# Tie-free first cluster by triangle products, and other places for side work, in attention with two MLPs

## The chip, the cores and the metric

The kernel runs on one core of a Trainium2 chip. The metric is the device time of one execution in microseconds (us), the median of several runs. The engines of the core run side by side, each through its own queue of instructions in order: TensorE (PE, matrix products and transposes), VectorE (DVE), ScalarE (ACT), GpSimd (POOL) and SyncE (SP, which here starts DMA transfers). They wait for each other by semaphores.

## The reference, cut to what matters

Attention over 16 heads (768 tokens of 64) in which a query sees only the keys of its own cluster (the first of 16 centroids with the largest similarity), then a Fourier mixing with norm and an MLP, then a gated MLP with a convolution over the tokens:

```python
q_assign = np.argmax(np.einsum('bhsd,hcd->bhsc', q_n, c_n), axis=-1)
k_assign = np.argmax(np.einsum('bhsd,hcd->bhsc', k_n, c_n), axis=-1)
mask = q_assign[:, :, :, None] == k_assign[:, :, None, :]
scores = np.where(mask, scale * np.matmul(q, k.transpose(0, 1, 3, 2)), -1000000000.0)
attn = np.exp(scores - np.max(scores, axis=-1, keepdims=True))
attn = attn / (np.sum(attn, axis=-1, keepdims=True) + 1e-09)
x = np.matmul(attn, v)                       # heads side by side: 2 x 768 x 512
u = x + np.real(np.fft.fft(np.fft.fft(x, axis=1), axis=2))
un = (u - mu) / np.sqrt(var + 1e-06)
x = u + np.maximum(un @ w_ch1, 0.0) @ w_ch2  # w_ch1 is 512 x 2048
h = np.maximum(x @ w_in, 0.0)                # w_in is 512 x 1024
conv_out = sum(conv_w[k] * hp[:, k:k + S, :] for k in range(3))
gate = 1.0 / (1.0 + np.exp(-conv_out))
return h * gate @ w_out
```

`np.argmax` takes the first of equal values, so where two clusters of a token are equally near, the one with the lower number counts.

## The kernel before

**Attention.** The 16 heads are taken as 8 pairs `m`; each head has 6 tiles of 128 tokens, which makes 96 tiles, and the loop at the end of the attention part runs one step `n` per tile. Step `n` issues the scores of tile `n + 8` (`score_max`: four products at L612 and L614 into a PSUM slot, and VectorE's negated row maximum at L617), then the transposed scores of tile `n` with mask and maximum in the product (`score_exp`: L649, L651, and ScalarE's exponential at L657), then the products with V of tile `n - 3` (`attn_v`, 18 products at L689). The probabilities are kept as two 16-bit parts: the high part by ScalarE (`prob_hi`, L669), the low part, which is the difference, by VectorE or GpSimd (`prob_lo`, L677); the set `LO_ON_DVE` lists the tiles whose low part VectorE makes. Scores and transposed scores take turns in three PSUM slots, so the transposed scores of tile `n + 1` go into the slot that the scores of tile `n + 8` leave: they wait for that tile's maximum on VectorE, and for whoever reads the slot's spare columns 384 to 512.

**Side work in the attention steps.** Everything else is put between these steps by hand, by `at(place, step, function)`; the places of a step in their order are `pre`, `mid` (which gets the score tile's slot and uses its spare columns), `late`, `aft`, `post` and `fill`. For the pair `m`, that begins at step `k = 12 m - 24`, these are: the similarities to the centroids (`prep_sims`), their turn and row maximum and the marks of equality with it (`sims_turn`, L472 and L482); then the first of equal marks, by a weight that falls with the cluster's number (`prep_first` L486, `prep_pick` L490, `prep_mark` L496), four transposes and two ScalarE copies of the one-hot marks (`prep_turn`, L511) and a DMA of them to DRAM; the high and low parts of q and k (`prep_hi` L536, `prep_lo`); and V's scale and two parts (`v_max`, `v_turn`, `v_step`, whose step 5 at L594 is V's low part on VectorE). The first steps of the Fourier mixing of the first batch and the conversion of the first weights (`ahead0` to `ahead3`, `first_split`) lie in the later steps.

**After the attention** the code gives only data, pools and priorities: a scheduler orders the instructions of each engine. MLP1 has 16 blocks `f` per batch (`mlp1_up`, `down`), the gated MLP has 8 (`mlp2_up`: products, ReLU, convolution on VectorE at L992 and L993, sigmoid, product with the gate, two parts; then `down`). Weights come as 64-bit words by DMA (`load_w`; `B_LOADS` lists the blocks of MLP1's second batch after which those of the gated MLP are asked for), VectorE converts them (L301 to L306), and they are scaled and split in two 16-bit parts (`split_16`: ScalarE, then VectorE at L947). `gate_in` measures the tokens (L1040 to L1042), turns them (L1065) and splits them (L1068). The outputs leave through a buffer `y` of three tiles.

## Time and profile before

| | |
|---|---|
| median of three runs | 680.25 us (678.62 to 681.44) |
| the profiled execution, its own time | 679.71 us |
| its span in the trace | 677.9 us |
| TensorE busy | 656.7 us, 97% |
| VectorE busy | 546.0 us, 81% |
| ScalarE busy | 420.1 us, 62% |
| GpSimd busy | 181.2 us, 27% |

The profile is of one execution; its time is 1.8 us more than its span, and 0.54 us less than the median. Busy shares are means over the whole span. A wait in the trace is the idle time of an engine just ahead of an instruction, with the instruction that came last of those that it waited for.

### The profile page before, as it was taken

The page shows a single profiled execution, that of the slowest core. Times are in us where ns is not written, and L with a number is a line of the kernel's source. Part 1 is how long each engine was busy: PE and PEld are TensorE (multiplying, and loading weights), DVE is VectorE, ACT ScalarE, POOL GpSimd, SP SyncE. Part 2 cuts the span into 40 slices and gives each one's busy share as a digit, 9 for nine tenths or more (in the row PEclk, how much of TensorE's full clock was granted, in tenths as well). Part 3 has the DMA queues.
Part 4 walks back from the last instruction along what each step waited for, and adds up shares of the span by engine and source line. Part 5 has one row for each costly group of instructions (what it writes and reads, how often), then busy time and mean ns, then how long its engine had stood idle before and what let it go on. Part 6 is the DMA issues. An engine that isn't in the chain of part 4 may idle for free.

```text
span 677.9 us, 12606 instructions
## 1 busy us (share of the span) xinstructions
PE 656.7 (97%) x5019; PEld 487.8 (72%) x5019; DVE 546.0 (81%) x884; ACT 420.1 (62%) x679; POOL 181.2 (27%) x153
## 2 busy tenths in 40 slices
PE   8999999898999999999999999999999999999996
PEld 4888888786989888899999996554555555555553
DVE  6989999989878999998599838997626399867663
ACT  6688888786667895566246644776436276655442
POOL 8376866676648742000011000000000000000000
PEclk9999999998999999999999999999999999999999
DMA  6678788682644530334013330333000000002002
GB/s 191 179 165 206 192 222 220 149 194 51 177 110 90 143 122 2 125 125 155 33 62 125 125 124 1 125 125 126 1 1 0 1 1 1 0 2 80 14 1 93
DMA packets 21542, 65.41 MB, mean 96 GB/s; under 512 B 4438, under 2 KB 7306, under 8 KB 18668
## 3 DMA queue, kind: packets, MB, share of 16 engines
q1 hardware_dynamic: 20476, 60.86, 31.3%
q0 software_dynamic: 1008, 3.75, 2.0%
q8 instruction: 39, 0.64, 0.4%
q14 instruction: 19, 0.16, 0.1%
HBM read 40.84 MB, written 5.58 MB: 68 GB/s over the span
## 4 chain that ended last, share of the span: by engine, by line
PE 65%; DVE 25%; ACT 4%; DMA 2%; issue 2%; SPq 1%; POOL 0%; DVEq 0%; ACTq 0%
PE acc L87 7%; PE acc L86 7%; PE acc L85 7%; PE up L85 5%; PE up L87 5%; PE up L86 5%; DVE m L617 4%; PE av L689 4%; PE s L612 3%; DVE p L677 3%; PE s L614 3%; PE t L649 3%; PE t L651 2%; PE u L85 2%; PE u L87 2%; PE u L86 2%
## 5 line engine op out<-in xcount | busy, mean ns | idle before, releaser
L677 POOL TENSOR_TENSOR p<-p,p 128x768 f16<-128x768 f32 x61 | 106.7, 1752 | 73.3 <-ACT p L669 32.8
L657 ACT ACTIVATE p<-t,cbias 128x768 f32<-128x768 f32 x93 | 83.6, 900 | 21.9 <-PE t L651 19.9
L617 DVE TENSOR_REDUCE m<-s 128x1 f32<-128x768 f32 x96 | 90.3, 946 | 5.6 <-PE s L614 3.5
L669 ACT CAST p<-p 128x768 f16<-128x768 f32 x90 | 74.7, 830 | 1.2
L689 PE MATMUL av<-V,p 128*128 128x65 f16 x1728 | 70.6, 195 | 1.0 <-POOL p L677 0.9
L689 PEld LDWEIGHTS <-p 128*128 128x128 f16 x1728 | 59.1, 98 | 16.3 <-issue 15.0
L649 PE MATMUL t<-X 128*128 128x384 f32 x192 | 54.7, 366 | 4.6 <-DVE m L617 4.1
L612 PE MATMUL s<-X 128*128 128x384 f32 x192 | 56.5, 376 | 1.8 <-DVE eq L482 0.5
L614 PE MATMUL s<-Y 96*128 96x384 f32 x192 | 49.7, 340 | 0.1
L651 PE MATMUL t<-Y 98*128 98x384 f32 x192 | 49.8, 340 | 0.0
L85 PE MATMUL u<-x,wb 128*128 128x384 f16 x128 | 41.7, 326 | 1.3 <-DVE h L989 0.9
L85 PE MATMUL up<-un,wa 128*128 128x384 f16 x128 | 41.8, 326 | 0.7 <-DVE x L1068 0.3
L677 DVE TENSOR_TENSOR p<-p,p 128x768 f16<-128x768 f32 x32 | 40.8, 1276 | 1.1 <-ACT p L669 1.1
L86 PE MATMUL up<-un,wa 128*128 128x384 f16 x128 | 41.7, 326 | 0.0
L87 PE MATMUL u<-x,wb 128*128 128x384 f16 x128 | 41.7, 326 | 0.0
L86 PE MATMUL u<-x,wb 128*128 128x384 f16 x128 | 41.7, 326 | 0.0
L87 PE MATMUL up<-un,wa 128*128 128x384 f16 x128 | 41.6, 326 | 0.0
L649 PEld LDWEIGHTS t<-X 128*128 128x128 f32 x192 | 31.3, 190 | 10.4 <-DVE m L617 7.1
L85 PE MATMUL up<-un,wha 128*128 128x384 f32 x112 | 38.0, 339 | 0.0
L86 PE MATMUL up<-un,wha 128*128 128x384 f32 x112 | 37.8, 337 | 0.0
L87 PE MATMUL up<-un,wla 128*128 128x384 f32 x112 | 37.7, 338 | 0.0
L265 POOL TENSOR_TENSOR rs<-rs,half 128x1 f32<-128x1 f32 x12 | 10.5, 905 | 100.5 <-DVE rs L260 92.5
(397 smaller groups left out, 1698.5 us busy)
## 6 DMA issues: line engine op xcount, KB each, us to landing
rawa<-w SPq DMA_DIRECT2D x14, 1024.0 KB, 4.7
rawb<-w SPq DMA_DIRECT2D x8, 1024.0 KB
raw<-qk SPq DMA_DIRECT2D x7, 768.0 KB, 4.3
X<-G SPq DMA_DIRECT2D x13, 384.0 KB, 3.7
Y<-G SPq DMA_DIRECT2D x13, 384.0 KB, 5.0
vraw<-v SPq DMA_DIRECT2D x8, 384.0 KB, 5.4
out<-y SPq DMA_DIRECT2D x12, 256.0 KB, 3.1
X<-G SPq DMA_DIRECT2D x14, 192.0 KB, 4.1
```

The costliest lines, as they stand in the source:

```text
L85: T.matmul(o, sH, mH, start=start, stop=False)
L86: T.matmul(o, sH, mL, start=False, stop=False)
L87: T.matmul(o, sL, mH, start=False, stop=stop)
L612: T.matmul(t[:, c, 0:384], X[:, 0, sl], X[:, 1, 384 * c:384 * c + 384], start=True, stop=False)
L614: T.matmul(t[:, c, 0:384], Y[0:96, 0, sl], Y[0:96, 1, 384 * c:384 * c + 384], start=False, stop=True)
L617: V.tensor_reduce(m6s[h][:, i:i + 1], t[:, :, 0:384], AX.XY, ALU.max, negate=True)
L649: T.matmul(t[:, c, 0:384], X[:, 1, sl], X[:, 0, 384 * c:384 * c + 384], start=True, stop=False)
L651: T.matmul(t[:, c, 0:384], Y[0:98, 1, sl], Y[0:98, 0, 384 * c:384 * c + 384], start=False, stop=True)
L657: A.activation(p, t[:, :, 0:384], AF.Exp, bias=cbias, scale=0.125)
L669: A.copy(p16[:, 0], p32s[n])
L677: eng.tensor_sub(p16[:, 1], p, p16[:, 0])
L689: T.matmul(o, p16[:, k, 128 * j:128 * j + 128], v16[:, i, h % 2, 65 * part:65 * part + 65], start=(i + j + k + part == 0), stop=(i == 5), ...
```

## The change

- **First of equal marks.** For the pairs 2 to 7, `prep_first`, `prep_pick`, `prep_mark` and `prep_turn` are replaced. `equal_turn` transposes the marks of equality themselves (four transposes, one ScalarE copy of 96x512). `equal_sole` multiplies them with a constant matrix `sole` (1 for the cluster itself, -1 for those of lower number in the same token block, 0 elsewhere), two products per half; a mark stays over 0 only where no lower cluster is marked. The half `a = 0` is read by ScalarE (ReLU with a factor), the half `a = 1` by VectorE (`tensor_scalar`), each 96x256. They hang on the score tiles of steps `k + 7`, `k + 8` and `k + 9`, where there were `prep_first` to `prep_mark` and, at `k + 11`, `prep_turn`. The DMA of the marks is issued two steps earlier.
- **Low parts.** `LO_ON_DVE` has 28 tiles where it had 32, and mostly others: 3 of 12 per pair up to the fifth. The low parts of q and k of pair 7 go from VectorE to GpSimd, `first_split` 3 from GpSimd to VectorE. In the last tiles, 90 and 92 are VectorE's instead of 91 and 94.
- **V.** The maximum of |V| of the pairs 0 and 6 is taken by ScalarE (absolute value with a sum as a bound) where it was VectorE's. V's low part and other side work stand at other steps, by the table `MOVED`, which overrides place and step in `at`.
- **MLP1's end.** The gated MLP's blocks of weights from the sixth on are asked for one block `f` later (`B_LOADS`); its scales, and the first splits, one block later too.
- **Gated MLP.** The splits of its later weights, and `measure` of the second batch, are held back by `issue_after` until the gate products of earlier blocks are issued. `y` has six buffers instead of three.

```diff
-LO_ON_DVE = ({n for n in range(54) if n % 12 in (2, 7, 8, 10)}
-             | {54, 56, 59, 61, 62, 68, 73, 76, 80, 83, 86, 87, 88, 91, 94})
+LO_ON_DVE = {4, 7, 8, 14, 16, 19, 20, 28, 31, 32, 40, 43, 44, 52, 55, 57, 59, 61, 67, 68, 72, 77, 80, 82, 85,
+             88, 90, 92}
+LO_BY_DVE = ()
+ABS_ON_ACT = (0, 6)
+MOVED = {
+    ("prep_sims", 2): ("post", 5),
...
+    ("v_step", 5, 5): ("fill", 56),
...
-    NA, NB, B_LOADS = (2, 7, 7), (3, 5), (1, 2, 4, 5, 7, 8, 9, 10)
+    NA, NB, B_LOADS = (2, 7, 7), (3, 5), (1, 2, 4, 5, 7, 9, 10, 11)
...
+        sole = ep.tile([96, NT, C], F16, name="sole")
+        G.memset(sole, -1.0)
...
+        def sole_part(op, fill_, p, t, c):
+            G.affine_select(sole, sole, [[t, NT], [c, C]], op, fill_, base=0, channel_multiplier=p)
+
+        def equal_turn(m, t):
+            p = t[0:96, :, 384:512].bitcast(F16)
+            e = eqs[m].rearrange("p (h a t) c -> p h a (t c)", h=2, a=2)
+            for a in range(2):
+                for h in range(2):
+                    T.transpose(p[:, a, 128 * h:128 * h + 128], e[:, h, a], ident16)
+            s = sts[m] = ep.tile([128, 384], F32, tag="st", bufs=1, name=f"eT{m}")[0:96, 0:256].bitcast(F16)
+            s = sts[m] = s.rearrange("p (a n) -> p a n", a=2)
+            A.copy(s, p)
+
+        def equal_sole(m, a, t):
+            p = t[0:96, :, 384:512]
+            for h in range(2):
+                T.matmul(p[:, h], sole.rearrange("p t c -> p (t c)"), sts[m][:, a, 128 * h:128 * h + 128],
+                         start=True, stop=True)
+            if a == 0:
+                o = ohTs[m] = ep.tile([96, 2, 2, 128], F32, tag="ohT", bufs=1, name=f"ohT{m}")
+                A.activation(o[:, 0], p, AF.Relu, scale=BIG)
+            else:
+                V.tensor_scalar(ohTs[m][:, 1], p, 0.0, 1.0, ALU.max, ALU.subtract)
+                d = ohD[m] = dr.tile([96, 2, 2, 128], F32, tag="ohd", name=f"ohd{m}")
+                nc.sync.dma_start(out=d, in_=ohTs[m])
...
-            V.tensor_reduce(sc[:, 0:1], vraws[m], AX.XYZ, ALU.max, apply_absolute_value=True)
+            if m in ABS_ON_ACT:
+                junk = V16s[m % 2].bitcast(BF16).rearrange("p t h e -> p (t h) e")[:, :, 0:64]
+                A.activation(junk, vraws[m].rearrange("p t h d -> p (t h) d"), AF.Abs, accum_out=sc[:, 0:1])
+            else:
+                V.tensor_reduce(sc[:, 0:1], vraws[m], AX.XYZ, ALU.max, apply_absolute_value=True)
...
-                at(fill, k + 6, prep_first, m, V if m == 6 else G)
-                at(fill, k + 7, prep_pick, m)
-                at(fill if m == 7 else late, k + (7 if m == 7 else 8), prep_mark, m)
...
-                at(mid, k + 11, prep_turn, m)
...
+                for f, n in zip(((equal_turn, m), (equal_sole, m, 0), (equal_sole, m, 1)),
+                                (8, 9, 11) if m == 2 else (k + 7, k + 8, k + 9)):
+                    at(mid, n, *f)
...
-                (V, G)[i // 2].tensor_sub(w[i], src, f32(w[i - 1]))
+                V.tensor_sub(w[i], src, f32(w[i - 1]))
...
-        V.tensor_mul(t, t, hc)
+        gate_op.append(V.tensor_mul(t, t, hc).ins)
...
-            ws_b[f + 1] = split_16(gp, "b", f + 1)
+            with tc.issue_after(gate_op[f - 2]):
+                ws_b[f + 1] = split_16(gp, "b", f + 1)
...
-                    y = gps[0].tile([128, 512], F32, tag="y", bufs=3, name=f"y{g}{t}")
+                    y = gps[0].tile([128, 512], F32, tag="y", bufs=6, name=f"y{g}{t}")
...
+            with tc.issue_after(gate_op[min(t, len(gate_op) - 1)]) if b else nullcontext():
+                measure_(t)
...
-            if (g, f) == (1, 11):
+            if (g, f) == (1, 12):
                 scales("b")
...
-            if g == 1 and f >= 12 and f < 12 + NB[0]:
-                ws_b[f - 12] = split_16(wbp[0], "b", f - 12)
+            if g == 1 and f >= 13 and f < 13 + NB[0]:
+                ws_b[f - 13] = split_16(wbp[0], "b", f - 13)
```

What this does to the order of VectorE's instructions is shown at three places. A row is line, operation, written tile <- read tiles, and shape; line numbers are those of the kernel it is of (the score maximum is L617 before and L786 after, the low part L677 and L847, V's low part L594 and L763).

VectorE in the attention, around the score tiles 62 to 65, where the marks of pair 6 are made. Before:

```order
L472 TENSOR_REDUCE mx6_2541<-cols6_2516 128x24
L482 TENSOR_TENSOR eq6_2543<-cols6_2516,mx6_2541 128x384
L617 TENSOR_REDUCE m6_10_2433<-s62_2533 128x1
L486 TENSOR_TENSOR eq6_2543<-eq6_2543,desc_135 128x384
L617 TENSOR_REDUCE m6_10_2433<-s63_2575 128x1
L677 TENSOR_TENSOR p16_54_2581<-p54_2553,p16_54_2581 128x768
L594 SCALAR_TENSOR_TENSOR V16_1_155<-vraw5_2149,vsc5_2355,V16_1_155 128x12x64
L490 TENSOR_REDUCE m26_2610<-eq6_2543 128x24
L617 TENSOR_REDUCE m6_10_2433<-s64_2612 128x1
L496 TENSOR_TENSOR oh6_2627<-desc_135,m26_2610 128x384
L697 TENSOR_SCALAR d8_2651<-av8_2413 128x6
L617 TENSOR_REDUCE m6_10_2433<-s65_2653 128x1
```

After:

```order
L611 TENSOR_REDUCE mx6_2548<-cols6_2528 128x24
L621 TENSOR_TENSOR eq6_2550<-cols6_2528,mx6_2548 128x384
L786 TENSOR_REDUCE m6_10_2443<-s62_2540 128x1
L786 TENSOR_REDUCE m6_10_2443<-s63_2585 128x1
L786 TENSOR_REDUCE m6_10_2443<-s64_2625 128x1
L847 TENSOR_TENSOR p16_55_2635<-p55_2604,p16_55_2635 128x768
L763 SCALAR_TENSOR_TENSOR V16_1_157<-vraw5_2164,vsc5_2347,V16_1_157 128x12x64
L867 TENSOR_SCALAR d8_2667<-av8_2423 128x6
L676 TENSOR_SCALAR ohT6_2632<-s65_2669 96x256
L786 TENSOR_REDUCE m6_10_2443<-s65_2669 128x1
```

The three operations on the marks (L486, L490, L496) are gone, V's low part and the one low part of this stretch stand behind the maximum of tile 64 instead of ahead of it, and the new reading of the products (L676) stands ahead of that of tile 65.

VectorE in MLP1's second batch, around block 6 (`h1_6` is the ReLU's low part of that block, `wb6` the gated MLP's seventh block of weights, `cw` the convolution's weights, `x0` the turned tokens). Before:

```order
L301 TENSOR_SCALAR wb6_6502<-rawb6_6503 128x1024
L302 SCALAR_TENSOR_TENSOR wb6_6502<-rawb6_6503,wb6_6502 128x1024
L971 SCALAR_TENSOR_TENSOR h1_6_6155<-up1_6_0_6156,h1_6_6155 128x384
L971 SCALAR_TENSOR_TENSOR h1_6_6155<-up1_6_1_6171,h1_6_6155 128x384
L304 SCALAR_TENSOR_TENSOR wb6_6502<-rawb6_6503,wb6_6502 128x1024
L301 TENSOR_SCALAR cw_4486<-craw_6512 128x24
L306 SCALAR_TENSOR_TENSOR wb6_6502<-rawb6_6503,wb6_6502 128x1024
L1068 TENSOR_TENSOR x0_5844<-xT03_6207,x0_5844 128x4
L302 SCALAR_TENSOR_TENSOR cw_4486<-craw_6512,cw_4486 128x24
L304 SCALAR_TENSOR_TENSOR cw_4486<-craw_6512,cw_4486 128x24
L1068 TENSOR_TENSOR x0_5844<-xT03_6207,x0_5844 128x4x127
```

After:

```order
L438 TENSOR_SCALAR cw_4499<-craw_6515 128x24
L439 SCALAR_TENSOR_TENSOR cw_4499<-craw_6515,cw_4499 128x24
L441 SCALAR_TENSOR_TENSOR cw_4499<-craw_6515,cw_4499 128x24
L1150 SCALAR_TENSOR_TENSOR h1_6_6168<-up1_6_0_6169,h1_6_6168 128x384
L443 SCALAR_TENSOR_TENSOR cw_4499<-craw_6515,cw_4499 128x24
L1150 SCALAR_TENSOR_TENSOR h1_6_6168<-up1_6_1_6184,h1_6_6168 128x384
L1252 TENSOR_TENSOR x0_5857<-xT03_6220,x0_5857 128x4
L438 TENSOR_SCALAR wb6_6580<-rawb6_6581 128x1024
L1252 TENSOR_TENSOR x0_5857<-xT03_6220,x0_5857 128x4x127
L439 SCALAR_TENSOR_TENSOR wb6_6580<-rawb6_6581,wb6_6580 128x1024
```

The conversion of `wb6` stands behind both parts of `h1_6` instead of ahead of and around them, the small `cw` conversions ahead, and the last piece of `x0` stands behind the first step of `wb6`.

VectorE at the start of the gated MLP (`h200` and `h201` are the ReLU products of the first two blocks, `cv00` and `cv01` their convolutions, `wb3` to `wb5` splits of later weights, `tok1` the measures of the second batch). Before:

```order
L947 SCALAR_TENSOR_TENSOR wb3_6987<-wb3_6225,scb_6643,wb3_6987 128x512 x2
L947 SCALAR_TENSOR_TENSOR wb4_7036<-wb4_6359,scb_6643,wb4_7036 128x512
L989 SCALAR_TENSOR_TENSOR h200_6856<-u000_6859,x0_5844 128x384
L947 SCALAR_TENSOR_TENSOR wb4_7036<-wb4_6359,scb_6643,wb4_7036 128x512
L1040 TENSOR_REDUCE tok10_7055<-U_68 128x1
L1040 TENSOR_REDUCE tok11_7070<-U_68 128x1
L989 SCALAR_TENSOR_TENSOR h200_6856<-u001_6874,x0_5844 128x384
L1041 TENSOR_SCALAR tok10_7055<-tok10_7055 128x1
L1041 TENSOR_SCALAR tok11_7070<-tok11_7070 128x1
L947 SCALAR_TENSOR_TENSOR wb5_7123<-wb5_6430,scb_6643,wb5_7123 128x512
L1042 TENSOR_SCALAR tok10_7055<-tok10_7055 128x1
L1042 TENSOR_SCALAR tok11_7070<-tok11_7070 128x1
```

After:

```order
L1168 SCALAR_TENSOR_TENSOR h200_6869<-u000_6872,x0_5857 128x384
L1168 SCALAR_TENSOR_TENSOR h200_6869<-u001_6887,x0_5857 128x384
L1171 SCALAR_TENSOR_TENSOR cv00_6902<-h200_6869,cw_4499,cv00_6902 128x768
L1168 SCALAR_TENSOR_TENSOR h201_6913<-u010_6916,x0_5857 128x384
L1172 SCALAR_TENSOR_TENSOR cv00_6902<-h200_6869,cw_4499,cv00_6902 128x768
L1168 SCALAR_TENSOR_TENSOR h201_6913<-u011_6931,x0_5857 128x384
L1161 MEMSET h202_6957 128x1
L1162 MEMSET h202_6957 128x1
L1174 TENSOR_TENSOR cv00_6902<-cv00_6902,hc00_6868 128x768
L1171 SCALAR_TENSOR_TENSOR cv01_6946<-h201_6913,cw_4499,cv01_6946 128x768
L1126 SCALAR_TENSOR_TENSOR wb3_7000<-wb3_6238,scb_6710,wb3_7000 128x512
L1177 TENSOR_TENSOR gL00_6909<-cv00_6902,gH00_6908 128x768
```

The two blocks' own work now comes first; the splits of `wb4` and `wb5` and the measures have left this stretch for later ones, and that of `wb3` stands in two halves behind the first block's gate product.

## Rows read from the trace of the kernel before

**Rows 1.** The profile's first part: span, then busy time, share and instructions per engine.
```profile
span 677.9 us, 12606 instructions
...
PE 656.7 (97%) x5019; PEld 487.8 (72%) x5019; DVE 546.0 (81%) x884; ACT 420.1 (62%) x679; POOL 181.2 (27%) x153
```

**Rows 2.** TensorE's waits: tile and line that waits <- engine, line: us, times, longest.
```profile
PE t L649 <- DVE m L617: 4.1, 3, 2.8
PE s L621 <- DVE m L617: 1.6, 1, 1.6
...
PE xT L1065 <- DVE h L971: 1.0, 1, 1.0
PE av L689 <- POOL p L677: 0.9, 1, 0.9
PE u L85 <- DVE h L989: 0.9, 1, 0.9
```

**Rows 3.** Timeline of TensorE, three steps: start, us, instruction, shapes, [wait ahead of it <- releaser].
```profile
102.22 0.59 PE L612 MATMUL s<-X 128*128 128x384 f32 x2
...
104.64 0.60 PE L612 MATMUL s<-X 128*128 128x384 f32 x2
...
106.70 0.59 PE L612 MATMUL s<-X 128*128 128x384 f32 x2
```

**Rows 4.** Timeline of VectorE ahead of TensorE's longest wait, pair 6.
```profile
154.72 1.54 DVE L677 TENSOR_TENSOR p<-p,p 128x768 f16<-128x768 f32 x1
156.18 2.41 DVE L594 SCALAR_TENSOR_TENSOR V<-vraw,vsc,V 128x768 f16<-128x768 f32 x1
...
158.97 0.94 DVE L617 TENSOR_REDUCE m<-s 128x1 f32<-128x768 f32 x1
```

**Rows 5.** That wait on TensorE, and the stretch behind it (window, length, PE, PEld, DVE, ACT, POOL busy, granted clock).
```profile
159.97 1.01 PE L649 MATMUL t<-X 128*128 128x384 f32 x2 [2.80 <-DVE m L617]
...
163.67 0.59 PE L649 MATMUL t<-X 128*128 128x384 f32 x2
...
159.95:163.36 3.41, 3.40 (x25) 3.09 (x26) 3.03 (x6) 1.62 (x2) 0.29 (x1) 0.50 0.00 0
```

**Rows 6.** Timeline of VectorE, two low parts in pair 5.
```profile
127.91 2.59 DVE L677 TENSOR_TENSOR p<-p,p 128x768 f16<-128x768 f32 x1
...
131.37 0.94 DVE L677 TENSOR_TENSOR p<-p,p 128x768 f16<-128x768 f32 x1
```

**Rows 7.** Groups by line: count | busy us, mean ns of one | idle ahead, releaser.
```profile
L677 POOL TENSOR_TENSOR p<-p,p 128x768 f16<-128x768 f32 x61 | 106.7, 1752 | 73.3 <-ACT p L669 32.8 <-issue 26.2 <-PE t L651 5.7
L657 ACT ACTIVATE p<-t,cbias 128x768 f32<-128x768 f32 x93 | 83.6, 900 | 21.9 <-PE t L651 19.9 <-POOL ev L115 0.7 <-POOL eq L486 0.6
L669 ACT CAST p<-p 128x768 f16<-128x768 f32 x90 | 74.7, 830 | 1.2
```

**Rows 8.** TensorE's wait in pair 3, and ScalarE's copy that is its root.
```profile
75.74 0.58 PE L649 MATMUL t<-X 128*128 128x384 f32 x2 [0.87 <-DVE m L617]
...
70.90 0.83 ACT L536 CAST G<-raw 128x768 fp32r<-128x768 f32 x1 [0.85 <-DMA Y<-G]
```

**Rows 9.** MLP1: the late VectorE step, and a load of weights in the chain.
```profile
462.71 1.23 DVE L302 SCALAR_TENSOR_TENSOR wb<-rawb,wb 128x1024 int32<-128x1024 int32 x1
463.85 1.02 DVE L971 SCALAR_TENSOR_TENSOR h<-up,h 128x384 f16<-128x384 f32 x2
...
456.74 5.22 DMA rawb<-w
```

**Rows 10.** Busy time in the first 50 us of the gated MLP (columns as in rows 5).
```profile
550.00:600.00 50.00, 48.22 (x277) 26.94 (x275) 44.83 (x97) 32.75 (x56) 0.00 (x0) 1.00 0.00 1
```

**Rows 11.** Timeline of VectorE at the end: the last two outputs that it makes.
```profile
672.49 0.75 DVE L1020 TENSOR_SCALAR y<-acc,ysc 128x512 f32<-128x512 f32 x1 [1.46 <-DMA out<-y]
...
673.89 0.75 DVE L1020 TENSOR_SCALAR y<-acc,ysc 128x512 f32<-128x512 f32 x1 [0.65 <-ACT y L1022]
```

**Rows 12.** Timeline of ScalarE at the start, ahead of the first transposed scores.
```profile
21.81 0.79 ACT L639 CAST Y<-first_max 2x768 fp32r<-2x768 f32 x1 [6.67 <-PE first_max L637]
```

More of the change, by code (lines that the diff above doesn't have):

```diff
@@ L411, in tile_net @@
         add_stack(G)
-        sq = ep.tile([128, D], F32, name="sq")
+        sq = ep.tile([128, 192], F32, tag="eq", bufs=1, name="sq")[:, 0:D]
         V.tensor_mul(sq, cn, cn)
@@ L705, in tile_net, with at @@
         LEAD, LAG = 8, 3
-        pre, mid, late, aft, post, fill = {}, {}, {}, {}, {}, {}
-        def at(where, step, *f):
+        pre, mid, mid2, late, aft, post, fill = {}, {}, {}, {}, {}, {}, {}
+        hooks = dict(pre=pre, mid=mid, mid2=mid2, late=late, aft=aft, post=post, fill=fill)
+        def at(where, step, *f, name=None):
+            key = (name or f[0].__name__, *(x for x in f[1:] if isinstance(x, int)))
+            if key in MOVED:
+                where, step = MOVED[key]
+                where = hooks[where]
             where.setdefault(step, []).append(f)
@@ L739, in tile_net @@
         at(fill, -3, first_split_max, 0)
+        for f in ((ALU.is_ge, 0.0, 1, -C, 0), (ALU.is_ge, 0.0, -1, C, 1), (ALU.not_equal, 1.0, -1, C, 1)):
+            at(fill, -4, sole_part, *f)
         at(fill, -2, prep_pick, 1)
@@ L774, in tile_net @@
         for name, where, n in plan:
-            at(where, n, first[name])
+            at(where, n, first[name], name=name)
         stat, root, scale, swap, low = norm(0, lambda name: slot(name)[:, 0], dp)
@@ L794, in ahead_start @@
             dst = ahead[q] = t[:, 2560 + 512 * q:3072 + 512 * q]
-            for n, op in zip(AHEAD_STEPS[5 * q:], from64(dst, raw)):
-                at(aft, n, op)
+            for i, (n, op) in enumerate(zip(AHEAD_STEPS[5 * q:], from64(dst, raw))):
+                at(aft, n, op, name=f"ahead{q}_{i}")
         def ahead_store(q):
@@ L897, in tile_net @@
                 score_exp(n)
+            for f in mid2.get(n, []):
+                f[0](*f[1:], tile_s)
             for f in late.get(n, []):
```

147 lines of the change are left out of this document (141 added, 6 removed).

## Prediction

> **What bounds the kernel now.** I read the profile's first part, then TensorE's waits, then the stretch around each wait on the engines it names. TensorE is busy 656.7 of 677.9 us [rows 1], so 21 us are all that filling its gaps can give, some of it at the start and end; a change gains here by the waits it takes from TensorE and loses by what it adds to TensorE's work or to the waits. In the attention VectorE is the usual releaser: the transposed scores wait 4.1 us for the score maximum, the turn of the maxima 1.6, one product with V 0.9 for GpSimd's low part [rows 2]. After it come single waits of about a microsecond for VectorE's h [rows 2]. No wait is spread over all steps: a free step is bound by TensorE and takes 2.06 us, from 104.64 to 106.70 [rows 3].
>
> The longest wait shows the pattern. At 159.97 TensorE had stood for 2.80 us [rows 5]; VectorE had made a low part of 1.54 us and V's low part of 2.41 us between two maxima, and the maximum that released TensorE began at 158.97 [rows 4]. TensorE then came back at the lower of its two clock levels: 0.50 granted over 3.41 us [rows 5].
>
> **The change part by part**, against the profiled 679.71 us.
>
> *A, products added.* The four transposes of the marks stay, at another step; four products per pair are new, 24 in all. No row of before has them. The nearest is a step that carries four transposes to 128 columns: 2.42 us (102.22 to 104.64) against 2.06 [rows 3], 0.09 each. That makes 24 x 0.09 = 2.2 us, all on the path, since TensorE bounds the step. The bounds are 1.0 (a product that overlaps its neighbours) and 4.5 (double, if the weights are loaded anew each time). I take 2.2, from the nearest shape. The matrix `sole` itself is made by GpSimd before the first step, beside the loads; were that cover gone, it is three passes over 96x96, under GpSimd's 1.75 us for 128x768 [rows 7].
>
> *B, waits that go.* In pair 6 nothing is left on VectorE between the maxima of tiles 62, 63 and 64; the low part and V's low part come behind. The wait of 2.80 goes, and with it the half clock: the next L649 came at 163.67, 3.70 us later, where a step takes 2.06 [rows 3, 5]; the 6-row turn in between takes a little, so 1.5. Together 4.3. Once that wait is gone, the next late thing there is the turn of the maxima, which is part of any head. In pair 5 the turn waited 1.6 [rows 2]; a low part on VectorE ahead of it took 2.59 us at 127.91, though another took 0.94 at 131.37 [rows 6]. The tiles on VectorE are now three per pair, and GpSimd has no marks to weigh. With the smaller wait of that pair (4.1 in all less 2.80 and 0.87 [rows 2, 8]) I count 2.0. The wait of 0.9 for GpSimd's low part in the tail [rows 2] goes, since tiles 90 and 92 are VectorE's now. Small starts of delay behind VectorE's low parts elsewhere give an estimated 1.1 (0.28 at each of four tiles whose low part leaves VectorE). Sum 8.3; bounds 5 (the turn of pair 5 still waits, the tail only changes tiles) and 9.
>
> First comes a rule that speaks against B. Two low parts of the same shape took 0.94 and 2.59 us on VectorE [rows 6], the longer one beside GpSimd's work. The Trainium skill says the same in "SBUF — State Buffer", section "SBUF: two separate sides": a VectorE instruction with two SBUF inputs and a GpSimd instruction exclude each other, the first to start for its whole length; the trace agrees (2.59 against 0.94). "Perfetto Trace Analysis", section "Optimizing Scalar/DVE Operations", draws the conclusion that offloading between the two might not help. By that rule the four low parts and the pair 7 differences handed to GpSimd would buy nothing, which is the first rival below.
>
> *C, waits that come.* The new reads sit on score tiles whose slot is wanted again. Behind the scores of tile n + 8 TensorE has about 1.6 us of other work (t of n, V's products of n - 3, s of n + 9) until it wants the slot; the maximum takes 0.95 of it, so some 0.65 are left for what stands ahead of the maximum. Before, one tile per pair (step k + 11) had such reads by ScalarE; now there are two by ScalarE (the marks, 96x512, and the half a = 0) and one by VectorE. ScalarE is busy 0.90 + 0.83 = 1.73 us of a step with the exponential and the high part [rows 7], and q's high part, 0.83 [rows 8], falls on step k + 8 too, so at k + 8 it has over 2.5 us to do in a step of 2.4. It will be late, by about half of one wait as pair 3 shows it (0.87, behind a late ScalarE copy [rows 8]). I take 0.5 for each of pairs 3 to 6, 2.0; bounds 0 and two waits of 0.87 for six pairs, 10.4. V's maximum on ScalarE at the start costs nothing: ScalarE was idle 6.67 us ahead of 21.81 [rows 12]. The old wait of pair 3 stays, since its root is a transfer.
>
> *D, MLP1.* VectorE's h of block 6 began at 463.85 behind a conversion of 1.23 us [rows 9], and TensorE waited 1.0 [rows 2]. It now stands ahead of wb6's conversion, and the 1.0 goes. But the transfer, 5.22 us [rows 9], is asked for one block later and, of the two buffers that take such loads in turn, gets the one that wb5's conversion leaves; I put its landing one transfer later, at 456.74 + 2 x 5.22 = 467. The last piece of x0 stands behind the conversion's first step and would be 1 to 2 us late. I take -0.2; bounds -1.4 (both gone) and +1.4 (a longer wait than before).
>
> *E, gated MLP.* The 0.9 for the first h of the gate [rows 2] goes, as the blocks' own work comes first. The held-back splits and measures do not vanish: VectorE is busy 44.83 of the first 50 us [rows 10], and so the 5 us that are put off meet a VectorE that has hardly 5 us free. I take -0.3; bounds -1 and +2.
>
> *F, end.* With six y buffers the last outputs wait for no transfer. VectorE stood 1.46 us for one at 672.49, and the last output began at 673.89 after 0.65 behind ScalarE's [rows 11], which is about 1.0 after the last product. So -1.0; bounds -0.65 and -1.46, all on the path, as only the transfer follows.
>
> Sum: +2.2 - 8.3 + 2.0 - 0.2 - 0.3 - 1.0 = -5.6, so 674.1 for an execution like the profiled one. The median of before is 0.54 above that one: 674.6.
>
> **Rivals.**
> - *R1, the shared path of VectorE and GpSimd eats the offload.* If each pair from 3 to 6 has one low part of VectorE that meets GpSimd's, it costs 1.65 (2.59 less 0.94 [rows 6]) less the 0.65 of slack, 1.0 each, 4.0 in all: 678.6. For it: GpSimd now makes four low parts more at 1.75 us [rows 7]. Against: the maxima come first in the new order, and fewer low parts are on VectorE.
> - *R2, VectorE is full behind the attention.* D and E at their upper ends, +1.6 and +2.3 against the sum: 678.5. For it: 44.83 of 50 us [rows 10]; against: only two waits of 1 us stand there now.
> - *R3, slower: ScalarE holds the slots.* If ScalarE comes more than 0.65 us late at k + 7 and at k + 8, both maxima of a pair are late as in pair 3 (0.87 [rows 8]). Twelve such waits are 10.4 in place of 2.0, and one that grows into a half-clock stretch adds 1.5 [rows 5]: 684.5. For it: 2.5 us of work in a 2.4 us step. Against: outside those two steps ScalarE has a third of a microsecond free per step, and the exponential may run behind without TensorE noticing at once.
> - *R4, better.* No lateness from C, D at -1.3, E at -1, F at -1.46: 4.3 less than the sum, 670.3.
> - That the marks don't do what they say is excluded: the order has no weighing on VectorE or GpSimd any more for pairs 2 to 7, as the part on pair 6 shows.
>
> **How the numbers follow.** Forecast 0.56, R1 0.14, R2 0.10, R3 0.11, R4 0.09. A difference under 0.5%, 3.4 us, is about what a measurement of this kernel can tell from no change, so faster is under 676.85 and slower over 683.65. Faster: the forecast and R4, less what of the forecast's own spread lies above (0.02): 0.63. Same: R1, R2 and that, 0.25 with rounding. Slower: R3, 0.12. The range leaves out R3 and the outer half of R4, and takes in R1 and R2 with both C and D somewhat over: 669.5 to 681.
>
> **What would show it.** A: a step with two `sole` products 0.15 to 0.2 longer, otherwise 2.06. B: no wait over 0.5 us near score tiles 62 to 66 and granted clock 1.0 there; no wait of the turn in pair 5. C: waits of t for the maxima of tiles 27, 28, 39, 40, 51, 52 with a ScalarE copy as releaser; none at all means R4, 0.8 and more each means R3. D: h1_6 prompt and x0's last piece waiting for wb6. E: no wait in the first two blocks, later ones behind splits. F: the last y right after the last product. The prediction is wrong if the waits of rows 2 stay with other names (R1), if new low clock stretches appear, or if the products cost TensorE over 4 us.

## The result, and the profile after

The changed kernel takes 674.34 us (median of 5 runs, 673.27 to 675.05) against 680.25 (5 runs, 677.98 to 681.44); the ratio is 0.992, 95% interval 0.9896 to 0.9944. The profiled executions have spans of 671.6 and 677.9 us. Their difference, 6.3, is what is explained here; that of the medians is 5.9. The profiled execution of the changed kernel is the fastest of its five, that of before lies 0.5 under its median.

The profile of the changed kernel begins as rows 1 do:

```profile
span 671.6 us, 12662 instructions
...
PE 656.6 (98%) x5043; PEld 486.7 (72%) x5043; DVE 525.4 (78%) x870; ACT 424.5 (63%) x683; POOL 184.1 (27%) x157
```

TensorE's busy time is the same with 24 instructions more, so by these sums the gain is idle time; but the busy time of before holds the 3.4 us at half clock [rows 5], which are gone, and that of after holds the new products. VectorE is busy 20.6 us less, far more than the marks that it no longer makes: 10.4 are low parts and 3.1 V's low parts, by the groups below. Where the gain lies is seen by laying the start of the same instruction in both traces side by side:

| start of | before | after | shift |
|---|---|---|---|
| t of tile 16 (pair 2's marks are out) | 58.22 | 59.30 | +1.1 |
| t of tile 44 | 124.96 | 125.98 | +1.0 |
| t of tile 46 (turn in pair 5) | 131.53 | 130.72 | -0.8 |
| t of tile 56 | 154.85 | 154.27 | -0.6 |
| t of tile 58 (behind the wait in pair 6) | 163.67 | 159.01 | -4.7 |
| t of tile 94, end of attention | 255.55 | 250.77 | -4.8 |
| a product of MLP1, first batch | 357.15 | 352.18 | -5.0 |
| a product of MLP1, second batch | 511.43 | 505.32 | -6.1 |
| the last product | 672.45 | 666.97 | -5.5 |
| end | 677.91 | 671.57 | -6.3 |

So the attention gives 5.0 (with the first products behind it), MLP1 1.1, the gated MLP takes 0.6 back, and the end gives 0.9.

TensorE's waits after, in the form of rows 2 (the first one is in pair 2, for a transfer that stands behind the marks' own; the others are for VectorE):

```profile
PE s L783 <- DMA Y<-G: 1.0, 1, 1.0
...
PE s L791 <- DVE m L786: 0.7, 4, 0.2
PE up L222 <- DVE d L869: 0.7, 1, 0.7
...
PE u L222 <- DVE h L1168: 0.5, 1, 0.5
```

Of the 4.1 us of t for the maximum 0.2 are left; the single wait of 1.6 of the turn, the 1.0 for h in MLP1 and the 0.9 for GpSimd's low part [rows 2] are gone. New are 1.0 for a transfer in pair 2 and four small waits of the turn.

Pair 6, VectorE's timeline, to be held against rows 4:

```profile
154.91 0.96 DVE L786 TENSOR_REDUCE m<-s 128x1 f32<-128x768 f32 x1 [1.01 <-ACT ohT L674]
155.79 0.95 DVE L847 TENSOR_TENSOR p<-p,p 128x768 f16<-128x768 f32 x1
156.65 1.01 DVE L763 SCALAR_TENSOR_TENSOR V<-vraw,vsc,V 128x768 f16<-128x768 f32 x1
157.58 0.15 DVE L867 TENSOR_SCALAR d<-av 128x6 f32<-128x6 f32 x1
157.66 0.41 DVE L676 TENSOR_SCALAR ohT<-s 96x256 f32<-96x256 f32 x1
157.99 0.94 DVE L786 TENSOR_REDUCE m<-s 128x1 f32<-128x768 f32 x1
```

A low part and V's low part still stand between two maxima, and ahead of the maximum that the turn of a head needs. But they take 0.95 and 1.01 us, where they took 1.54 and 2.41 [rows 4]. What ran on GpSimd beside them differs. Before:

```profile
153.67 4.09 POOL L677 TENSOR_TENSOR p<-p,p 128x768 f16<-128x768 f32 x2
157.91 2.33 POOL L545 TENSOR_TENSOR G<-raw,G 128x768 fp32r<-128x768 f32 x1
```

After:

```profile
153.77 1.65 POOL L847 TENSOR_TENSOR p<-p,p 128x768 f16<-128x768 f32 x1
157.20 2.15 POOL L710 TENSOR_TENSOR G<-raw,G 128x768 fp32r<-128x768 f32 x1 [1.77 <-ACT G L701]
```

GpSimd is idle from 155.42 to 157.20 now, and both steps of VectorE begin in that gap. The sums over the whole attention point the same way, in the groups by line, the first two of before, the others of after:

```profile
L677 DVE TENSOR_TENSOR p<-p,p 128x768 f16<-128x768 f32 x32 | 40.8, 1276 | 1.1 <-ACT p L669 1.1
L594 DVE SCALAR_TENSOR_TENSOR V<-vraw,vsc,V 128x768 f16<-128x768 f32 x8 | 12.1, 1513 | 0.7 <-ACT V L592 0.6
```

```profile
L847 DVE TENSOR_TENSOR p<-p,p 128x768 f16<-128x768 f32 x28 | 30.4, 1088 | 0.8 <-ACT p L839 0.8
...
L763 DVE SCALAR_TENSOR_TENSOR V<-vraw,vsc,V 128x768 f16<-128x768 f32 x8 | 9.0, 1122 | 1.4 <-ACT V L761 1.3
```

A low part costs 1088 ns in the mean instead of 1276, V's 1122 instead of 1513, though their shapes are the same.

What makes such a step long can be counted. The 14 traces (the two kernels and the twelve runs below) hold 549 low parts, V's low parts and additions of 128x771 on VectorE. The 300 that began while GpSimd was idle (its issues of transfers left out) took 0.94 to 1.02 us, also where a step of GpSimd began meanwhile. The other 249 began during a step of GpSimd, and 183 of them took more than 1.05, up to 2.62; each of these 183 ended 0.81 to 0.83 after that step of GpSimd did. The kernel before has 18 of them, the changed one 10.

### The profile page after: what moved, and what is told of

Same layout as the page of the kernel before. It is cut to its first block, busy times and chain, and to the rows that moved or that the text cites. A ratio compares the mean times of both kernels' runs of the same rounds, so it can differ in the third digit from the quotient of the medians.

```text
span 671.6 us, 12662 instructions
## 1 busy us (share of the span) xinstructions
PE 656.6 (98%) x5043; PEld 486.7 (72%) x5043; DVE 525.4 (78%) x870; ACT 424.5 (63%) x683; POOL 184.1 (27%) x157
## 4 chain that ended last, share of the span: by engine, by line
PE 67%; DVE 19%; ACT 5%; DMA 4%; issue 2%; SPq 1%; POOL 0%; ACTq 0%; DVEq 0%
PE acc L224 7%; PE acc L222 7%; PE acc L223 7%; PE av L859 5%; PE up L222 5%; PE up L224 5%; PE up L223 5%; PE s L781 4%; PE t L819 4%; PE s L783 3%; PE t L821 3%; DVE m L786 2%; DMA Y<-G 2%; PE u L222 2%; PE u L224 2%
## 5 line engine op out<-in xcount | busy, mean ns | idle before, releaser
L847 POOL TENSOR_TENSOR p<-p,p 128x768 f16<-128x768 f32 x65 | 110.7, 1712 | 63.4 <-ACT p L839 37.3
L786 DVE TENSOR_REDUCE m<-s 128x1 f32<-128x768 f32 x96 | 90.7, 948 | 20.0 <-PE s L783 7.7
L223 PE MATMUL acc<-wb,gH 128*128 128x512 f16 x96 | 36.4, 379 | 0.0
L224 PE MATMUL acc<-wa,h 128*128 128x512 f16 x96 | 36.4, 379 | 0.0
L222 PE MATMUL acc<-wa,h 128*128 128x512 f16 x96 | 36.4, 379 | 0.0
```

The costliest lines, as they stand in the source:

```text
L222: T.matmul(o, sH, mH, start=start, stop=False)
L223: T.matmul(o, sH, mL, start=False, stop=False)
L224: T.matmul(o, sL, mH, start=False, stop=stop)
L786: V.tensor_reduce(m6s[h][:, i:i + 1], t[:, :, 0:384], AX.XY, ALU.max, negate=True)
L847: eng.tensor_sub(p16[:, 1], p, p16[:, 0])
```

## The experiments

Shifts are read as in the table above, against the profiled execution of the kernel that was edited; TensorE's wait is read in that stretch. All but the last are single runs, on three chips. Beside them the kernel before took 686.63, 681.21 and 682.31 in single runs, and 677.21 to 682.66 in eleven runs of one session. So a total alone says little here, and an experiment is read by the stretch that its edit touches.

**What the products cost.** The changed kernel with each product made twice:

```diff
-            for h in range(2):
+            for h in (0, 1, 0, 1):
```

> The changed kernel with every product with the triangle made twice (48 instead of 24; the second writes the same result again). Theory (term A): each product costs TensorE 0.09 us on the path, so the 24 more cost 2.2 us, and each of the 12 steps that hold them is 0.18 longer. Rival: they are hidden in gaps that TensorE has in these steps anyway, and the whole moves by less than 0.7; or each loads its weights anew and costs double, 4.5.

The execution took 676.51 us, its span is 3.2 longer. But the products themselves are cheap. Between the starts of two of them lie 0.055 us, in every one of the 12 steps, so that 24 more are 1.3. The two that the changed kernel has in a step make the time from the scores' last product to t 0.08 longer than in a step without: 1.0 for all 12 steps, at my lower bound and not at 2.2. The other 1.9 of this run are mostly two waits that stand elsewhere: 0.6 for a transfer at 144.9, and 1.1 for VectorE at 181 and 182. Term A was over-sized by double, and the experiment's total alone would have hidden it.

**Queue position or neighbour: pair 6.** The kernel before with V's low part of pair 5 one step later:

```diff
-            at(pre if m == 6 else fill if m == 1 else aft, lo, v_step, m, 5)
+            at(pre if m == 6 else fill if m in (1, 5) else aft, lo + (m == 5), v_step, m, 5)
```

> The kernel before with one edit: the low part of V of pair 5 stands one step later, behind the maximum of tile 64. The marks of pair 6 are still weighed and picked on VectorE between the maxima. Theory (term B, pair 6): the queue on VectorE ahead of that maximum is what made the wait of 2.80 us; without V's 2.41 us some 0.4 of it is left, the clock keeps its upper level, and 3.5 to 4.3 us of the 4.3 come from this move alone. Rival: the marks (1.40 and 0.54 us) are the cause; then over 1.5 us of wait stay, and the half-clock stretch with it.

679.71 us, as before. VectorE and TensorE there:

```profile
158.82 2.59 DVE L594 SCALAR_TENSOR_TENSOR V<-vraw,vsc,V 128x768 f16<-128x768 f32 x1
```

```profile
158.35 0.62 PE L649 MATMUL t<-X 128*128 128x384 f32 x2 [0.47 <-DVE m L617]
...
162.40 0.27 PE L621 MATMUL s<-ident,m 128*6 128x128 f32 x1 [1.73 <-DVE m L617]
```

The wait of 2.80 became 0.47, as the theory had it, but V's low part still took 2.59 us, one maximum further on, and the turn waited 1.73 for that; the clock fell to half from 163.7 on. The shift over both waits is only -0.7. Neither theory held: the move passed the same long step on to the next maximum. That left its length.

The same run shows that a wait of the kernel before need not come in each execution. In pair 5, where the edit changes nothing, the turn did not wait 1.6, and 1.7 was gained (shift +2.3 at tile 45, +0.6 at tile 46). The low part of 2.59 [rows 6] took 0.94 there. The first line is GpSimd's step of before, the others are of this run:

```profile
127.64 2.04 POOL L545 TENSOR_TENSOR G<-raw,G 128x768 fp32r<-128x768 f32 x1 [1.73 <-ACT G L536]
```

```profile
130.20 0.94 DVE L677 TENSOR_TENSOR p<-p,p 128x768 f16<-128x768 f32 x1
```

```profile
130.19 2.65 POOL L545 TENSOR_TENSOR G<-raw,G 128x768 fp32r<-128x768 f32 x1 [1.98 <-ACT G L536]
```

Before, GpSimd began 0.27 ahead of VectorE, and VectorE's step was long; here the two began within 0.01, and GpSimd's was. (The run lost 2.3 ahead of that place, mostly behind transfers, so its total is that of before.)

The kernel before with tile 55's low part on VectorE, which changes nothing on VectorE ahead of the maximum in question and takes away only what ran on GpSimd beside V's low part:

```diff
-             | {54, 56, 59, 61, 62, 68, 73, 76, 80, 83, 86, 87, 88, 91, 94})
+             | {54, 55, 56, 59, 61, 62, 68, 73, 76, 80, 83, 86, 87, 88, 91, 94})
```

> The kernel before with the low part of tile 55 on VectorE instead of GpSimd. On VectorE nothing changes ahead of the maximum of tile 64; the low part of 55 stands behind it. On GpSimd the second of two low parts that ran beside V's low part of pair 5 is gone. Theory (what ran beside it on GpSimd made V's low part take 2.41 us): V's low part takes 1.0 to 1.3, the wait at 159.97 falls from 2.80 to 1.1 to 1.6. Rival (queue position: three long steps ahead of one maximum, whatever runs beside): V's low part stays over 2 us, or the wait over 2.4.

VectorE, TensorE and the window that was at half clock [rows 5]:

```profile
156.44 1.54 DVE L677 TENSOR_TENSOR p<-p,p 128x768 f16<-128x768 f32 x1
157.90 1.01 DVE L594 SCALAR_TENSOR_TENSOR V<-vraw,vsc,V 128x768 f16<-128x768 f32 x1
158.83 0.54 DVE L490 TENSOR_REDUCE m<-eq 128x24 f16<-128x384 f16 x1
159.30 0.94 DVE L617 TENSOR_REDUCE m<-s 128x1 f32<-128x768 f32 x1
160.16 1.71 DVE L496 TENSOR_TENSOR oh<-desc,m 128x384 f16<-128x384 f16 x1
```

```profile
160.29 0.62 PE L649 MATMUL t<-X 128*128 128x384 f32 x2 [1.41 <-DVE m L617]
```

```profile
159.95:163.36 3.41, 2.33 (x26) 1.85 (x26) 3.41 (x5) 1.96 (x3) 1.51 (x1) 1.00 0.00 0
```

V's low part takes 1.01 in place of 2.41, the wait falls from 2.80 to 1.41, and the clock stays at its upper level. The shift over tile 58 is -1.6, since the turn now waits 1.1 behind the marks (L496 took 1.71 beside GpSimd's next step) and the low part added. (The run as a whole, 679.39, is hardly shorter: it lost 1.7 before, in pairs 2 and 3, mostly to transfers, where the edit does nothing.) The price is shown by this: 1.4 us of a wait of 2.8 came from one step of GpSimd beside one of VectorE. The Trainium skill, "SBUF — State Buffer", section "SBUF: two separate sides", has the loser of such a pair blocked until the other is done. The trace of before agrees: GpSimd's two steps ended at 153.67 + 4.09 = 157.76, and V's low part, begun at 156.18, ended at 158.59, 0.8 later; alone it takes 1.01.

**The list, and the moves.** The changed kernel with the old list; the kernel before with the new list; the changed kernel without the moves:

```diff
-LO_ON_DVE = {4, 7, 8, 14, 16, 19, 20, 28, 31, 32, 40, 43, 44, 52, 55, 57, 59, 61, 67, 68, 72, 77, 80, 82, 85,
-             88, 90, 92}
+LO_ON_DVE = ({n for n in range(54) if n % 12 in (2, 7, 8, 10)}
+             | {54, 56, 59, 61, 62, 68, 73, 76, 80, 83, 86, 87, 88, 91, 94})
```

> The changed kernel with the list of the kernel before for the low parts that VectorE makes (32 tiles, four of twelve per pair), all else as changed. Theory (term B, pair 5 and tail): which tiles VectorE takes, and what GpSimd does beside them, is worth about 3 us: the turn in pair 5 waits 1 to 1.6 again, the tail 0.9, and low parts of 1.5 to 2.6 us come back on VectorE; total +2 to +4. Rival R1 (the shared path eats the offload whatever the list): the total stays within 1 us. Other rival: the products alone made the room, and only the tail's 0.9 returns.

677.78 us, span +4.5. The size is a little over the theory's +4, and the places are others: the turn in pair 5 does not wait again, and the tail's wait of 0.9 is back but costs 0.2. Instead 0.8 goes over pairs 2 to 5, 0.7 in pair 6, and 2.3 at one place in pair 7, where TensorE waited for VectorE in the Fourier mixing and then had 3.4 us at half clock:

```profile
181.56 0.62 PE L781 MATMUL s<-X 128*128 128x384 f32 x2 [1.12 <-DVE Zy L303]
```

> The kernel before with one edit: the changed kernel's list of the 28 tiles whose low part VectorE makes. The marks, V's low part and all else stay. Theory (the list and the removal of the marks work together): with the marks still between the maxima, the wait in pair 6 stays over 1.5 us and the half-clock stretch with it, and only pair 5 (1.5 to 2.0 us) and the tail's 0.9 are gained: -1 to -3. Rival: the list is the whole gain, and the attention is about 4.5 us shorter, as it was 4.5 longer with the old list in the changed kernel.

681.08 us, span +1.4 against the profiled execution of the kernel before, and inside the spread of its runs. Pair 5 gained 1.9, but the unchanged list gained 1.7 there in the run with V's step moved, so this is not shown to be the list's. Pair 6 gained 2.0. Lost were 3.3 at tile 24, 1.1 at tile 76 and 0.7 in the tail. The loss at tile 24 is a transfer of maxima that came late, with half a clock behind it; whether the list made it late, one run doesn't tell:

```profile
80.78 0.59 PE L651 MATMUL t<-Y 98*128 98x384 f32 x2 [1.94 <-DMA Y<-mr]
```

In pair 6 the wait moved on, and did not stay as the theory had it: V's low part is past (1.48), and now the addition of two halves of the Fourier mixing is long (2.05 at 164.77) and the maximum behind it late:

```profile
167.74 0.61 PE L649 MATMUL t<-X 128*128 128x384 f32 x2 [2.33 <-DVE m L617]
```

```diff
-MOVED = {
-    ("prep_sims", 2): ("post", 5),
...
-}
+MOVED = {}
```

> The changed kernel with an empty table of moves: products, list, V's maxima on ScalarE and all behind the attention as changed, the side work at the steps that the kernel before has. Theory: with the marks gone from VectorE, V's low part of pair 5 alone ahead of the maximum of tile 64 costs a wait of 0.5 to 1.5 us, not 2.8; with other small ones the attention is 1 to 3 us longer than in the changed kernel. Rival: the moves are what fits the rest to the new list; without them low parts of over 1.5 us on VectorE return in number, and over 4 us of the gain is lost, with a half-clock stretch.

681.38 us, span +8.1: the rival. V's low part took 17.3 us in eight instead of 9.0, seven of them over 1.2; pair 6 lost 4.1 to such an addition, with half a clock behind it:

```profile
164.37 2.06 DVE L146 TENSOR_TENSOR ev<-ev,ev 128x771 f32<-128x771 f32 x1
166.36 1.81 DVE L652 TENSOR_REDUCE m<-s 128x1 f32<-128x768 f32 x2
```

```profile
167.35 0.82 PE L685 MATMUL t<-X 128*128 128x384 f32 x2 [2.34 <-DVE m L652]
```

The addition takes 0.95 in the changed kernel (at 161.70). The losses at tile 76 (1.1) and 94 (1.6) are those that the list alone had too. Without the moves, then, neither the list (681.08) nor list and products (681.38) gained in these runs; the products alone were not run.

**Where the reading stands.** The changed kernel with the second half of the marks at k + 11, and with the halves swapped:

```diff
-                                (8, 9, 11) if m == 2 else (k + 7, k + 8, k + 9)):
+                                (8, 9, 11) if m == 2 else (k + 7, k + 8, k + 11)):
```

> The changed kernel with the second half of the marks (read by VectorE) two steps later in the pairs 3 to 7, at step k + 11, where pair 2 has it. Theory: the changed kernel's new waits of the turn of the maxima (four of about 0.3 us, in the pairs 3 to 6) come from VectorE's 0.41 us of reading ahead of the sixth maximum of a head, and go; but the DMA of the marks leaves two steps later, and the move of q and k that stands behind it in the queue lands about 1 us late as in pair 2 (wait of 0.99 at 58.8), in up to five pairs: total +2 to +4. Rival: the transfers have slack in the other pairs; total -1.

680.82 us, span +7.5, more than expected and by another way; 0.7 of it came ahead of the first edited step. The four turn waits went, and of the transfers of q and k one more made TensorE wait, 0.35 (one of maxima, 1.2 at 253.2, is of the kind that other runs have too). But t waited for VectorE's small steps at k + 11 (0.2 to 0.9, four times), and in pair 6 the addition of the Fourier mixing met GpSimd (2.58 at 163.49): t waited 2.40 and the half clock lasted 6.8 us.

```profile
163.49 2.58 DVE L280 TENSOR_TENSOR ev<-ev,ev 128x771 f32<-128x771 f32 x1
166.00 0.41 DVE L676 TENSOR_SCALAR ohT<-s 96x256 f32<-96x256 f32 x1
166.33 0.94 DVE L786 TENSOR_REDUCE m<-s 128x1 f32<-128x768 f32 x1
```

```diff
-            if a == 0:
+            if a:
...
-                for f, n in zip(((equal_turn, m), (equal_sole, m, 0), (equal_sole, m, 1)),
+                for f, n in zip(((equal_turn, m), (equal_sole, m, 1), (equal_sole, m, 0)),
```

> The changed kernel with the two halves of the marks swapped: VectorE's reading (0.41 us) at k + 8, ScalarE's at k + 9, ahead of the sixth maximum of a head, for which the turn waits. Theory (term C): the four waits of the turn of 0.33 us are VectorE's reading standing ahead of that maximum on its own queue; ScalarE's copy runs beside VectorE, and they fall under 0.15: -0.7 to -1.3 in all. Rival: whoever reads, the maximum waits until the reading is done; then they stay or grow, 0 to +1.5, as ScalarE has 1.73 us of other work per step.

676.07 us, span +2.8. Neither in full: of the four waits of the turn those in pairs 5 and 6 went, as the theory had it, that of pair 4 stayed (0.19), and that of pair 3 grew to 0.78, since ScalarE's reading came late there and the maximum waited 0.93 for it. Pair 2 gained 1.3, as its marks left earlier; pair 6 lost 3.1 to the same addition (2.58 at 160.31), t waiting 2.11 with half a clock behind it, and 1.2 more went behind tile 70. So the turn waits where the reading ahead of its maximum is late, whoever reads, and what an edit does to the steps behind it weighs more than these waits.

**Pair 2's transfer.** The changed kernel with two edits:

```diff
+            if h == 4:
+                stack_move(h, 1)
             stack_mask(h)
-            stack_move(h, 1)
+            if h != 4:
+                stack_move(h, 1)
...
+    ("attn_out", 0, 2): ("late", 11),
```

> The changed kernel with the last move of q and k of head 4 issued ahead of the mask's (which waits for the marks), and VectorE's output step of head 0 at step 11 instead of 10, behind the reading of pair 2's marks. Theory: the changed kernel's wait of 0.99 us at 58.8, for the transfer of that move, is its place in the queue behind the marks; it goes, and the attention is 0.7 to 1.1 us shorter from step 16 on. Rival: the transfers share one bandwidth, and the mask then comes late instead: 0 to +0.5.

673.72 us; -0.9 from tile 16 on, as expected. It comes back at tile 65, +1.1. ScalarE's maximum of V there waits for V, which is late by the clock, and what stands behind it on ScalarE is late with it:

```profile
176.60 0.84 ACT L742 ACTIVATE V<-vraw 128x768 bf16<-128x768 f32 x1 [2.25 <-DMA vraw<-v]
```

```profile
178.53 0.62 PE L785 MATMUL s<-X 128*128 128x384 f32 x2 [0.64 <-DVE Zy L304]
```

That wait was 1.00 in the changed kernel and cost nothing; it is the one edit that I had not priced (the maximum of pair 6 on ScalarE).

**Behind the attention.** The holding back taken out, then the loads and the buffers as before:

```diff
-            with tc.issue_after(gate_op[f - 2]):
-                ws_b[f + 1] = split_16(gp, "b", f + 1)
+            ws_b[f + 1] = split_16(gp, "b", f + 1)
...
-            with tc.issue_after(gate_op[min(t, len(gate_op) - 1)]) if b else nullcontext():
-                measure_(t)
+            measure_(t)
```

> The changed kernel without the holding back in the gated MLP: its later splits and the measures of the second batch may be ordered as the scheduler likes, as in the kernel before. Theory (term E): the waits of 0.9 and 0.5 us in the first two blocks return, the ones of the changed kernel at 566 to 595 us (together about 1.2) go; from the gate's start to the last product the stretch becomes 0.4 to 1.0 us shorter than in the changed kernel, since held-back work met a full VectorE. Rival: the holding back is a gain, and the stretch becomes over 0.3 us longer.

673.86 us. From the first product of the gated MLP to the last product it is 0.64 shorter than in the changed kernel, as the theory said; the old waits are back, and cost less than what the holding back had cost:

```profile
PE u L222 <- DVE h L1168: 0.8, 1, 0.8
PE acc L222 <- ACT gH L1176: 0.5, 1, 0.5
```

```diff
-    NA, NB, B_LOADS = (2, 7, 7), (3, 5), (1, 2, 4, 5, 7, 9, 10, 11)
+    NA, NB, B_LOADS = (2, 7, 7), (3, 5), (1, 2, 4, 5, 7, 8, 9, 10)
...
-                    y = gps[0].tile([128, 512], F32, tag="y", bufs=6, name=f"y{g}{t}")
+                    y = gps[0].tile([128, 512], F32, tag="y", bufs=3, name=f"y{g}{t}")
```

> The changed kernel with the old steps of the gated MLP's loads and with three y buffers again; two edits 130 us apart, read each in its own stretch. Theory (term D as the trace of the changed kernel shows it): the wait for h of block 6 in MLP1, 1.0 us, comes back, so that MLP1 is 0.7 to 1.4 us longer; (term F): the last two outputs wait for a transfer again, and from the last product to the end it is 0.8 to 1.0 us longer. Rivals: D: it was the order of the conversions, not the loads, and MLP1 keeps its time; F: the end is set by the last transfer, and stays within 0.3.

676.16 us. MLP1 loses 1.1, with the waits of before (0.7 for h and 0.3 for x), and from the last product to the end it is 0.87 longer, with the transfer ahead of an output again:

```profile
PE xT L1249 <- DVE h L1150: 0.7, 1, 0.7
PE up L222 <- DVE x L1252: 0.3, 1, 0.3
```

```profile
668.93 0.75 DVE L1200 TENSOR_SCALAR y<-acc,ysc 128x512 f32<-128x512 f32 x1 [1.45 <-DMA out<-y]
```

**Four edits together.** The changed kernel with the two edits on pair 2, V of pair 6 loaded three steps earlier, and the splits held back but not the measures:

```diff
-            load, top, hi, lo = {1: (2, 5, 12, 13), 2: (8, 13, 17, 19), 6: (62, 64, 67, 71), 7: (68, 71, 74, 74)}.get(
+            load, top, hi, lo = {1: (2, 5, 12, 13), 2: (8, 13, 17, 19), 6: (59, 64, 67, 71), 7: (68, 71, 74, 74)}.get(
...
-            with tc.issue_after(gate_op[min(t, len(gate_op) - 1)]) if b else nullcontext():
-                measure_(t)
+            measure_(t)
```

> The changed kernel with the two edits on pair 2 (order of the stack moves, output step one later), V of pair 6 loaded three steps earlier, so that ScalarE's maximum of it need not wait for its transfer, and the measures of the second batch no longer held back (the splits still are). Theory: the changed kernel loses 0.9 at pair 2, which comes back as a wait for that transfer at 178 us unless V is there earlier; and 0.64 by holding back, of which the measures (waits of the turn at 566 and 587 us) are the larger part. Expected 672.8 (-1.5), span 670.1. Rival: the earlier load of V delays the moves of q and k behind it in the queue: no gain over the changed kernel.

671.12 us (median of 6, 670.71 to 672.14), ratio to the kernel before 0.9882, interval 0.9861 to 0.9902. The changed kernel's interval begins at 0.9896, so the two overlap a little. The times themselves don't, as its fastest run is 673.27; but they are of two sessions, and in this one the kernel before took 679.37 and not 680.25. The profiled execution, the slowest of the six, has a span 1.1 shorter than that of the changed kernel. The gain in pair 2 is kept to the end of the attention (-0.75 at tile 88; V's maximum of pair 6 waits for nothing now), but for 0.7 that went behind a late transfer of maxima at 245.9, which several runs have in other sizes. The gated MLP is 1.4 shorter than in the changed kernel, so holding the splits is worth some 0.8 (1.4 against 0.64) and holding the measures was the loss, as far as two single traces tell. One wait of TensorE is left there:

```profile
PE u L223 <- DVE h L1172: 0.5, 1, 0.5
```

## Why the prediction was right, point by point

The time, 674.3, is the forecast's 674.6, and it came out faster by 5.9 as against 5.6. The parts are less good than the sum.

- *A, products: over-sized.* 2.2 was forecast from the transposes of a step; the products' own starts are 0.055 apart and add 1.0 in all. The step that failed is the choice of row: the longer step that I divided by four transposes holds other delays too. Its four transposes start 0.055 to 0.058 apart as well, which is about 0.2 of its 0.36.
- *B, waits that go: right in size, wrong in the reason.* Pair 6 gave 4.1 of 4.3 and pair 5 1.8 of 2.0; but pair 5's wait is not in every execution of the kernel before (above), so luck has a part in that gain. Nor is the half clock of pair 6 in every one: four of the eleven later runs of the kernel before have a mean granted clock of 0.998, which leaves no room for 3.4 us at half. They still have spans of 676.2 to 677.6, so the gain does not hang on it. Only 0.24 came in the tail: the wait for GpSimd went, and one of 0.7 for VectorE stands behind it (up, above). The small delays, for whose 0.28 each no row was named, may be the 0.3 to 0.4 that went at each of four places (tiles 12 to 14, 24 to 26, 36 to 38 and 48 to 51). The reason given, too much in VectorE's queue ahead of a maximum, was half the matter. Moving V's step alone passed the wait on; 1.4 of the 2.8 was the length that one step gets from its neighbour on GpSimd. The wait of pair 3, which I had said stays since its root is a transfer, went (0.9 between tiles 22 and 23). The maximum that released it [rows 8] stood behind a low part that GpSimd's step from 71.82 to 73.66 made long; it stands behind the maximum now, and is short. Before, then after:

```profile
72.50 1.98 DVE L677 TENSOR_TENSOR p<-p,p 128x768 f16<-128x768 f32 x1 [0.57 <-ACT p L669]
```

```profile
74.37 1.16 DVE L847 TENSOR_TENSOR p<-p,p 128x768 f16<-128x768 f32 x1 [0.18 <-ACT p L839]
```

- *The rule against the change.* It was weighed as R1, that offloading between VectorE and GpSimd buys nothing; the Trainium skill, "Perfetto Trace Analysis", section "Optimizing Scalar/DVE Operations", says that it might not help. Here GpSimd makes four low parts more (184.1 us busy against 181.2), and VectorE's total falls by 20.6. With the list alone it fell by 8.9 (to 537.1), but the one run was not shorter. So the offload did free VectorE; that TensorE gained by it hung on where the steps stand. R1 did not come.
- *C, waits that come: right in size, by others.* 2.0 was forecast behind ScalarE's copies. There are four waits of the turn, 0.7 in idle time and 0.3 each by the time between starts, behind VectorE's reading, and 1.0 in pair 2 for a transfer behind the marks' DMA. ScalarE's lateness (R3) is not to be seen in TensorE's waits, though VectorE's maximum at 154.91 (above) waited 1.01 for ScalarE's reading, and so its queue was late ahead of the turn. None of the waits of t came that I had named as a sign of C; their absence was to mean R4, whose 670.3 did not come either.
- *D, MLP1: under-sized.* -0.2 was forecast, -1.1 came. The weights landed as forecast, at 461.6, which with the shift of 5.0 is 466.6 by the old trace (forecast 467). The step that failed is what that costs: the last piece of x0 stood behind it, but TensorE was in the products ahead of it until 462.5 and lost 0.3 by the time between starts, not 1 to 2.
- *E, gate: right that it is no gain, wrong in sign.* -0.3 against +0.6, inside the bounds. The one part is a gain (splits), the other a loss (measures), which the profile of before could not tell apart.
- *F, end: right.* -1.0 forecast, -0.86 came; the last output of VectorE follows the last product at once:

```profile
667.38 0.75 DVE L1200 TENSOR_SCALAR y<-acc,ysc 128x512 f32<-128x512 f32 x1 [0.54 <-PE acc L224]
```

A was 1.2 and D 0.9 too gloomy, E 0.9 too good; so the sum hit better than its terms, 0.7 short by the profiled executions (6.3 against 5.6) and 0.3 by the medians. Five runs of the changed kernel lie within 1.8 us, five of the kernel before within 3.5 and eleven later ones within 5.5, so a hit of 0.3 is luck in part.

Open is why transfers of maxima and of q and k come late by 0.4 to 1.9 us in some runs and not in others; no run here was made for it.

## What to carry to other kernels

Where two engines lengthen each other's steps, price a step by what runs beside it: look for the same line at two durations, and ask what the other engine did at the longer one. Here a long step moved past one wait was handed to the next while its neighbour stayed, so moves and the division of work are worth trying together. A wait in one trace can be gone in the next without an edit, when two steps change places by a few tenths of a microsecond; a second trace of the unchanged kernel tells which waits are steady. After a gain, the things that are late by the clock, transfers above all, are the next to wait for: a gain ahead of them is kept only if they are started earlier too.

## What the runs showed of the hardware

- A VectorE step that reads two tensors in SBUF (low part, V's low part, the addition of 128x771) took 0.94 to 1.02 when GpSimd was idle at its start. When it began during a step of GpSimd and took over 1.05 us, it ended 0.81 to 0.83 after that step did (183 times in 14 traces), having taken up to 2.62. Two that began within 0.1 of GpSimd's start took 0.94 and 1.00, and GpSimd's ran on (2.65 and 2.03). A maximum, which reads PSUM, took 0.88 to 0.96 in all 14 traces.
- TensorE's granted clock fell to 0.50, its lower level, for 3.4 us (once 6.8) during or after waits of 1.12, 1.73, 1.94, 2.11, 2.34, 2.40 and 2.80 us, and did not after one of 2.33 in the kernel with the new list alone, nor after 1.41, 1.60 and 1.61. So a wait's length alone did not decide it here. A stretch of 3.4 us at half cost about 1.5 (in the run without the moves, shift +3.8 at tile 60 and +5.3 at tile 61).
